# Eight v tiles of the second batch move into unused columns of the q and k buffers, and are loaded earlier

## The chip, the cores and the metric

The kernel runs on one core of a Trainium2 chip. The metric is the time of one execution on the device in microseconds (us). Three executions of the kernel before took 538.85, 540.19 and 541.0 us; the median, 540.19, is the time before.

## The reference

Three stages, each feeding the next. Inputs are random normal numbers; most are scaled up by 8.

```python
# attention: B=2, H=8, S=768, D=64; block 32, window 16
k_sum = k.reshape(B, H, 24, 32, D).max(axis=3)
v_sum = v.reshape(B, H, 24, 32, D).mean(axis=3)
scores_l = q @ k^T / 8, kept where |i - j| < 16
scores_s = q @ k_sum^T / 8 + log(32)
a = softmax([scores_l, scores_s]);  x = a @ [v, v_sum]      # -> 1536 x 512
# experts: 8 of them, 512 -> 1024 -> 512; one per token
do = x @ w_skip > 0;  e = argmax(x @ w_gate);  g = softmax(x @ w_gate)[e]
x[do] += g * (relu(x @ w1[e]) @ w2[e])
# feed-forward 512 -> 2048 -> 512
h = x @ w_in;  out = (h >= 1 ? h : h <= -1 ? 0 : (h + 1)^2 / 4) @ w_out
```

## The kernel before, in words

**Stages.** The program first does the attention with the routing of the tokens (`attention`), which goes on into the block of the first expert; then the other experts; then the feed-forward layer. In attention every engine executes its instructions in the order in which the code lists them. Buffers are guarded by semaphores that the framework derives from the regions read and written: an instruction waits for the earlier ones that touch what it touches.

**Attention units.** The 24 units of attention are counted through both batches: 0 to 11 for batch 1 (index b = 0 in the code), 12 to 23 for batch 2 (b = 1). A unit is one token tile of 128 queries and half of the heads. A token tile t consists of two blocks j = 2t and 2t + 1 of 64 queries, each with a window of 96 keys (64 of its own and 16 at either side) and 24 block sums. So unit 18 (batch 2, t = 3, first half of the heads) and unit 19 read v tiles 6 and 7 of batch 2. In batch 1 the first six units go through tiles 0, 1, 2 twice.

In step i of the loop TensorE transposes the probabilities of unit i + 1 (`stage_t`, L449), makes the scores of unit i + 3 (`stage_s`, L437), and multiplies the probabilities of unit i by v (`stage_pv`, L466, tile `xo`). VectorE takes the row maximum of the scores (`nm`, L439), ScalarE the exponentials (`p`, L442), ScalarE copies the transposed probabilities (`pts`, L451), VectorE divides by the sum and writes the token tile (`den`, L469; `x`, L471). Then `run_todo(i)` (L780) issues what the table `todo` lists for step i: loads, routing of a finished token tile (`r1` to `r5`), weight fetches and pieces of weight splits.

**v tiles.** A v tile holds 120 rows (96 keys, 24 block sums) by 8 heads by 66 columns: 64 of v, two that are 1 for the keys and 32 for the sums, whose product is the divisor. `load_v` (L381, its DMA is L385) loads the keys of one tile from `v`, 192 KB; it is issued by SP. There are NV = 6 buffers `vw`; tile j of either batch goes to `vw[j % 6]`, so that each load after the first six waits for the last unit that reads the buffer's old tile. In batch 1 the block sums are put there by `spread` (L370). For batch 2 they go through DRAM: `store_vs` (L373, GpSimd) writes them to `vs_d`, and `put_vs` (L375, its DMA is L376, SP) copies them into a tile's last 24 rows. That is done for the first six tiles of batch 2; the other six find the same sums in their buffer. The v loads of batch 2 stand at steps 8 to 19, one per step.

**q and k.** Each pair of heads of each batch has a buffer `pb` of 2976 columns for its q and k blocks; its zeros are set by `init_pair`. These buffers have the places ("w00" to "w13") which later hold the split expert weights, of 4096 columns each. Pairs 4 to 7, of batch 2, have "w10" to "w13".

**SP's queue.** SP issues all of these loads in the order of the code; when one has to wait for a buffer, those behind it wait too. For batch 2 its order around the change is: a v load and a copy of sums per step; at step 11 a register load (`top_reg`) of a number that VectorE works out at step 10; at steps 12 to 15 the four fetches of the first expert's weights (`fetch`, L129, 1 MB each) behind the v load of that step; at steps 18 and 19 the list of the first block's tokens (`load_ids`, L216) and the gather of their rows on GpSimd (L219); at steps 20 to 22 the next expert's fetches.

**Routing.** A finished token tile gets its places in the experts' lists; GpSimd scatters indices (`ids_d`, L556) and rows (`xf`, L224) to DRAM. The tokens live in a ring of 7 buffers `x`, so a new tile's first write (L471) waits for the scatter of the tile seven places earlier. The split of a weight (`hi` on ScalarE, L139; `lo` on VectorE, L145) is done in pieces in steps 15 to 24.

Of the kernel before, what the change touches and what calls it, by code (L numbers as in the profile page):

```python
# [8 lines left out]
F32 = mybir.dt.float32  # L9
# [15 lines left out]
NV = 6  # L25
# [15 lines left out]
def tile_net(ctx, tc, q, k, v, w_skip, w_gate, w1, w2, w_in, w_out, out):  # L41
    nc = tc.nc
# [3 lines left out]
    NT = B * S // 128  # L46
    cp = ctx.enter_context(tc.tile_pool(name="cons", bufs=1))
    wp = ctx.enter_context(tc.tile_pool(name="w", bufs=1))
# [236 lines left out]
    def attention(actx):  # L285
# [24 lines left out]
                masks.append(m)  # L310


        pb = {}
        for i, tag in enumerate(("w02", "w03", "w00", "w01", "w10", "w11", "w12", "w13")):
            t = wp.tile([128, 2976], F32, tag=tag, name=f"pb{i}")
            pb[i] = t[:, 0:1536].rearrange("p (j c) -> p j c", c=128), t[:, 1536:2976].rearrange("p (j c) -> p j c", c=120)
        vw = [per.tile([120, 8, 66], F32, name=f"vw{i}") for i in range(NV)]

        def init_pair(eng, i):
            tq, tk = pb[i]  # L320
            eng.memset(tq[0:64, :, 64:128], 0.0)
            eng.memset(tq[64:128, :, 0:64], 0.0)
            eng.memset(tk[:, 0, 0:16], 0.0)
            eng.memset(tk[:, 11, 80:96], 0.0)

        def pbuf(b, hp):
            return pb[4 * b + hp]
# [45 lines left out]
            nc.gpsimd.dma_start(out=vs_d[96 * c:96 * c + 96], in_=vs[c])  # L373

        def put_vs(b, j, hs=slice(0, 8)):  # L375
            nc.sync.dma_start(out=vw[j % NV][96:120, hs],  # L376
                              in_=vs_d.rearrange("(b h n) d -> b n h d", b=B, h=H)[b, :, hs])

        vtile = {}

        def load_v(b, j):  # L381
            t = vw[j % NV]
            lo, hi = max(0, 64 * j - 16), min(S, 64 * j + 80)
            r0 = lo - (64 * j - 16)
            nc.sync.dma_start(out=t[r0:r0 + hi - lo, :, 0:64], in_=v[b, :, lo:hi].rearrange("h s d -> s h d"))  # L385
            vtile[b, j] = t
# [35 lines left out]
        def units(i):  # L422
            b, t, a = i // 12, (i % 12) // 2, i % 2
            if i < 6:
                t, a = i % 3, i // 3
            return b, t, a, [(2 * a + c, 2 * t + e) for c in range(2) for e in range(2)]

        def stage_s(i):
            b, _, _, us = units(i)
            s = ps.tile([128, 4, 120], F32, tag="s", name="s", bufs=3)  # L430
            t = units(i)[1]
            mask = masks[1 if t == 0 else 2 if t == 5 else 0]
            nc.tensor.matmul(s.rearrange("p (c e) k -> p c e k", c=2), identb,
                             mask.unsqueeze(1).to_broadcast([128, 2, 2, 120]), start=True, stop=False)
            for u, (hp, j) in enumerate(us):
                tq, tk = pbuf(b, hp)
                nc.tensor.matmul(s[:, u], tq[:, j], tk[:, j], start=False, stop=u == 3)  # L437
            nm = wk.tile([128, 4], F32, tag="nm", name="nm", bufs=3)
            nc.vector.tensor_reduce(out=nm, in_=s, axis=AX.X, op=ALU.max, negate=True)  # L439
            p = wk.tile([128, 4, 120], F32, tag="p", name="p")  # L440
            for u in range(4):
                nc.scalar.activation(out=p[:, u], in_=s[:, u], func=AF.Exp, bias=nm[:, u:u + 1], scale=1.0)  # L442
            st["p", i] = p
# [12 lines left out]
        def stage_pv(i):  # L456
            b, t, a, us = units(i)
            pts = st.pop(("t", i))
            tt = 6 * b + t
            if a == 0:  # L460
                xt[tt] = next(xnext)
            xo = ps.tile([128, 4, 66], F32, tag="xo", name="xo", bufs=2)
            for u, (hp, j) in enumerate(us):
                par = j % 2
                for h in range(2):
                    nc.tensor.matmul(xo[64 * par:64 * par + 64, 2 * (u // 2) + h], pts[:, u, 64 * h:64 * h + 64],  # L466
                                     vtile[b, j][:, 2 * hp + h, :], start=True, stop=True)
            den = wk.tile([128, 4], F32, tag="den", name="den")
            nc.vector.tensor_scalar(out=den, in0=xo[:, :, 64], scalar1=1e-9, scalar2=None, op0=ALU.add)  # L469
            nc.vector.reciprocal(out=den, in_=den)  # L470
            nc.vector.tensor_tensor(out=xt[tt][:, 256 * a:256 * a + 256].rearrange("p (s d) -> p s d", d=64),  # L471
                                    in0=xo[:, :, 0:64], in1=den.unsqueeze(2).to_broadcast([128, 4, 64]), op=ALU.mult)
# [257 lines left out]
        def at(i, f, *a):  # L730
            todo[i].append(lambda: f(*a))

        for t in range(3, NT):
            for e in range(2):
                b, j = t // 6, 2 * (t % 6) + e
                i = 2 * t - 4 + (e or t == 3)
                at(i, load_v, b, j)
                if b and j < NV:
                    at(i, put_vs, 1, j)
        groups = {2: (0, 1, 2), 5: (3, 4, 5), 6: (6,), 8: (7, 8), 10: (9, 10), 11: (11,)}  # L740
        of = {t: g for g in groups.values() for t in g}
        for t in range(NT):
            i = 2 * t + 1 if t > 2 else t + 3
# [49 lines left out]

        load_qk(0, 0), load_qk(0, 1)
        load_v(0, 0)
        load_vsum(0)
        load_v(0, 1)
        load_qk(0, 2)
        load_v(0, 2)
# [46 lines left out]
        route_consts(tri, per.tile([128, E * CAP // 128 + 2], I32, name="sent"), per.tile([128, 8], I32, name="ii"))  # L846
        for i in range(4, 8):
            init_pair(nc.gpsimd, i)
        stage_s(3)
        stage_pv(2)  # L850
        stage_s(4)
# [16 lines left out]
        t, = end = groups[NT - 1]  # L868
# [455 lines left out]
    with ExitStack() as actx:  # L1324
        with tc.manual_schedule():
            attention(actx)
# [38 lines left out]
```

## Time and profile before

| | |
|---|---|
| three executions | 538.85, 540.19, 541.0 us |
| the profiled execution | 538.99 us, its span 537.3 us |
| TensorE busy | 492.9 us (92%) |
| VectorE busy | 356.4 us (66%) |
| ScalarE busy | 286.1 us (53%) |
| GpSimd busy | 109.9 us (20%) |
| mean granted TensorE clock | 0.961 |

The profiled execution is one run; the span goes from its first to its last instruction, and its own time is 1.7 us longer. An engine's busy time is a mean over stages of different kinds: attention takes roughly the first 130 us, the experts follow to about 250, the feed-forward layer is the rest. In the rows below, PE is TensorE, DVE is VectorE, ACT is ScalarE, POOL is GpSimd, and SPq is the queue of SP. A clock of 1.00 is TensorE at full speed.

### The profile page before, as it was taken

How to read it: one execution, taken by the hardware profiler on the slowest of the kernel's cores; microseconds unless marked ns; L12 is line 12 of the kernel's file. 1: busy time of each engine (PE TensorE's matmuls, PEld its weight loads, DVE VectorE, ACT ScalarE, POOL GpSimd, SP SyncE). 2: the span in 40 equal slices, each digit the busy share in tenths (PEclk: the TensorE clock that was granted, in tenths of full speed). 3: DMA queues.
4: the chain of work that ended last, by engine and by line, in shares of the span. 5: the costliest groups of instructions: out<-in, count | busy, mean ns of one | idle time of the engine just before them, and what ended most of it. 6: DMA issues, size and time to landing. Idle time of an engine off the chain costs nothing.

```text
span 537.3 us, 7783 instructions
## 1 busy us (share of the span) xinstructions
PE 492.9 (92%) x2742; PEld 401.2 (75%) x2742; DVE 356.4 (66%) x714; ACT 286.1 (53%) x512; POOL 109.9 (20%) x159
## 2 busy tenths in 40 slices
PE   6887979687989999986899999999999999999994
PEld 3676868586778888854678888888888888888883
DVE  6667675869588879989989999543333444333341
ACT  6575546563457686773567777633233343332341
POOL 8506431603544231332000000020000002000002
PEclk9799999877889999999899999999999999999998
DMA  9997517997289887998425566020000002000002
GB/s 206 224 211 182 102 38 185 237 248 206 70 296 364 277 290 264 314 342 309 160 78 205 192 230 220 21 80 0 1 0 1 0 1 79 1 0 1 1 0 84
DMA packets 66760, 76.83 MB, mean 143 GB/s; under 512 B 31046, under 2 KB 48486, under 8 KB 66328
## 3 DMA queue, kind: packets, MB, share of 16 engines
q1 hardware_dynamic: 63256, 67.99, 43.1%
q0 software_dynamic: 3456, 8.26, 4.6%
q8 instruction: 23, 0.38, 0.3%
q14 instruction: 25, 0.20, 0.2%
HBM read 69.55 MB, written 8.12 MB: 145 GB/s over the span
## 4 chain that ended last, share of the span: by engine, by line
PE 43%; issue 33%; DVE 12%; ACT 6%; DMA 3%; POOL 1%; SPq 1%; POOLq 0%; ACTq 0%; DVEq 0%
PE hf L1146 9%; PE hp L935 5%; PE yp L959 5%; PE o L1189 3%; PE o L1187 3%; PE s L437 3%; PE o L1188 3%; DMA vw<-in_v_dram 3%; DVE w L145 3%; PE tph L945 2%; PE hp L264 2%; POOL out_dram L1199 1%; PE xo L466 1%; PE pt L449 1%; PE lp L492 1%
## 5 line engine op out<-in xcount | busy, mean ns | idle before, releaser
L1146 PE MATMUL hf<-xh,w 128*128 128x512 f32 x384 | 128.3, 397 | 1.2 <-ACT xh L257 0.7
L1146 PEld LDWEIGHTS hf<-xh,w 128*128 128x128 f32 x384 | 72.5, 190 | 18.0 <-ACT w L1111 1.0
L145 DVE TENSOR_TENSOR w<-stg,w 128x1024 fp32r<-128x1024 f32 (+1 forms) x72 | 76.5, 1096 | 6.8 <-ACT w L139 6.8
L1187 PE MATMUL o<-w,g 128*128 128x512 f32 x192 | 77.2, 402 | 2.2 <-ACT g L1171 2.2
L1188 PE MATMUL o<-w,g 128*128 128x512 f32 x192 | 76.5, 398 | 0.0
L1146 PE MATMUL hf<-xl,w 128*128 128x512 f32 x192 | 75.5, 393 | 0.0
L1189 PE MATMUL o<-w,g 128*128 128x512 f32 x192 | 71.3, 399 | 0.0
L139 ACT CAST w<-stg 128x1024 fp32r<-128x1024 f32 (+1 forms) x72 | 65.0, 958 | 3.1 <-PE hp L935 1.5
L1156 ACT ACTIVATE c<-c,scal 128x512 f32<-128x512 f32 x32 | 23.2, 724 | 76.7 <-DVE c L1155 76.6
L1199 POOL DMA_INDIRECT out_dram<-ob,perm x12 | 11.8, 983 | 254.2 <-DVE ob L1198 165.0
L1166 DVE TENSOR_TENSOR hf<-hf,c 128x512 f32<-128x512 f32 x48 | 33.5, 698 | 39.5 <-ACT hf L1164 37.7
L1155 DVE TENSOR_SCALAR c<-hf 128x512 f32<-128x512 f32 x32 | 22.1, 692 | 42.2 <-PE hf L1146 42.2
L1172 DVE TENSOR_TENSOR g<-hf,g 128x512 fp32r<-128x512 f32 x48 | 33.1, 690 | 22.7 <-ACT g L1171 22.6
L1187 PEld LDWEIGHTS o<-w,g 128*128 128x128 f32 x192 | 36.4, 189 | 10.8 <-ACT g L1171 2.7
L1171 ACT CAST g<-hf 128x512 fp32r<-128x512 f32 x48 | 28.1, 586 | 28.4 <-DVE hf L1166 28.2
L1189 PEld LDWEIGHTS o<-w,g 128*128 128x128 f32 x192 | 36.6, 191 | 8.7
L1146 PEld LDWEIGHTS hf<-xl,w 128*128 128x128 f32 x192 | 36.3, 189 | 8.8 <-DVE xl L258 0.7
L1188 PEld LDWEIGHTS o<-w,g 128*128 128x128 f32 x192 | 36.7, 191 | 8.3
L442 ACT ACTIVATE p<-s,nm 128x120 f32<-128x120 f32 x96 | 26.8, 362 | 29.3 <-DVE nm L439 21.3
L224 POOL DMA_INDIRECT xf<-x,ids x10 | 24.6, 2456 | 64.5 <-DVE x L967 63.3
L959 PE MATMUL yp<-w,hT 128*128 128x512 f32 x128 | 34.6, 407 | 2.3 <-DVE w L145 2.3
L935 PE MATMUL hp<-w,xT 128*128 128x512 f32 x128 | 34.2, 416 | 2.1 <-DVE xT L924 1.3
(211 smaller groups left out, 825.1 us busy)
## 6 DMA issues: line engine op xcount, KB each, us to landing
stg<-in_moe_w_dram SPq DMA_DIRECT2D x32, 1024.0 KB, 7.6
raw<-in_moe_w_in_dram SPq DMA_DIRECT2D x14, 512.0 KB, 3.7
raw<-in_moe_w_out_dram SPq DMA_DIRECT2D x14, 512.0 KB
vw<-in_v_dram SPq DMA_DIRECT2D x20, 192.0 KB, 6.0
x<-xf SPq DMA_DIRECT2D x12, 264.0 KB, 6.2
raw<-in_k_dram SPq DMA_DIRECT2D x16, 192.0 KB, 3.9
raw<-in_q_dram SPq DMA_DIRECT2D x16, 192.0 KB, 4.2
vraw<-in_v_dram SPq DMA_DIRECT2D x4, 768.0 KB, 9.0
```

The lines of the kernel that those rows point to most:

```text
L139: copy(out=part(wset[p, c // 2][0], c % 2, i, pieces), in_=part(stage[p, c], 0, i, pieces))
L145: eng.tensor_tensor(out=lo, in0=part(stage[p, c], 0, i, pieces), in1=hi.bitcast(F32), op=ALU.subtract)
L442: nc.scalar.activation(out=p[:, u], in_=s[:, u], func=AF.Exp, bias=nm[:, u:u + 1], scale=1.0)
L935: nc.tensor.matmul(hp, xT[:, kk], w[:, kk, 512 * f:512 * f + 512], start=(kk == 0 and w is hi), stop=(kk == 3 and w is lo))
L959: nc.tensor.matmul(yp, hT[:, kk], w[:, kk], start=(kk == 0 and w is hi), stop=(kk == 7 and w is lo))
L1146: nc.tensor.matmul(hp, w[:, 128 * kk:128 * kk + 128], a[:, kk], start=(n == 0), stop=(n == 11))
L1166: nc.vector.tensor_tensor(out=hp, in0=hp, in1=c, op=ALU.add)
L1171: nc.scalar.copy(out=gh, in_=hp)
L1172: nc.vector.tensor_tensor(out=gl, in0=hp, in1=gh.bitcast(F32), op=ALU.subtract)
L1187: nc.tensor.matmul(ops[ch][t], gh[:, a], hi, start=(f == 0), stop=False)
L1188: nc.tensor.matmul(ops[ch][t], gh[:, a], lo, start=False, stop=False)
L1189: nc.tensor.matmul(ops[ch][t], gl[:, a], hi, start=False, stop=(f == NF - 1))
```

## The change

The buffers of pairs 4 to 7 grow from 2976 to 4032 columns. Each of these four tails holds two v tiles, so there are eight more. Tiles 0 to 7 of batch 2 go to the tails (those of pairs 6 and 7 first), tiles 8 to 11 to `vw[0]` to `vw[3]`. `init_tails`, on GpSimd right behind `init_pair` of the same buffers, sets the columns of ones in all eight and 16 rows of zeros in tile 0. The v loads of batch 2 stand at step 5 (tiles 0 and 1), 6 (2, 3), 7 (4, 5), 8 (6 to 9) and 10 (10, 11). All twelve tiles get their sums by `put_vs`, three tiles at each of steps 8 to 11. Batch 1 keeps its buffers and the steps of its loads.

```diff
-        pb = {}
+        pb, tails = {}, []
         for i, tag in enumerate(("w02", "w03", "w00", "w01", "w10", "w11", "w12", "w13")):
-            t = wp.tile([128, 2976], F32, tag=tag, name=f"pb{i}")
+            t = wp.tile([128, 4032 if i > 3 else 2976], F32, tag=tag, name=f"pb{i}")
             pb[i] = ...
+            if i > 3:
+                tails += [t[0:120, 2976 + 528 * n:3504 + 528 * n].rearrange("p (h d) -> p h d", d=66) for n in range(2)]
         vw = [per.tile([120, 8, 66], F32, name=f"vw{i}") for i in range(NV)]
+        vbuf = {(0, j): vw[j % NV] for j in range(12)}
+        vbuf.update({(1, j): (tails[4:] + tails[:4] + vw)[j] for j in range(12)})
+
+        def init_tails():
+            for t in tails:
+                nc.gpsimd.memset(t[0:96, :, 64:66], 1.0)
+            nc.gpsimd.memset(vbuf[1, 0][0:16], 0.0)
...
-            nc.sync.dma_start(out=vw[j % NV][96:120, hs],
+            nc.sync.dma_start(out=vbuf[b, j][96:120, hs],
...
-            t = vw[j % NV]
+            t = vbuf[b, j]
...
-        for t in range(3, NT):
+        for t in range(3, 6):
             for e in range(2):
-                b, j = t // 6, 2 * (t % 6) + e
-                i = 2 * t - 4 + (e or t == 3)
-                at(i, load_v, b, j)
-                if b and j < NV:
-                    at(i, put_vs, 1, j)
+                at(2 * t - 4 + (e or t == 3), load_v, 0, 2 * t + e)
+        for j in range(12):
+            at(5 + j // 2 if j < 8 else 6 + (j - 8) // 2 * 2 + 2, load_v, 1, j)
+            at(8 + j // 3, put_vs, 1, j)
...
         for i in range(4, 8):
             init_pair(nc.gpsimd, i)
+        init_tails()
```

## Rows read from the trace of the kernel before

**Rows 1.** The chain of waits, 76 to 160 us: start, us, what.
```profile
94.25 14.19 DMA vw<-in_v_dram
```
**Rows 2.** Timeline of TensorE, 60 to 150: start, us, instructions [idle before <-releaser].
```profile
103.83 0.42 PE L466 MATMUL xo<-vw,pts 120*64 120x66 f32 x4
108.48 1.14 PE L466 MATMUL xo<-vw,pts 120*64 120x66 f32 x12 [4.24 <-DMA vw<-in_v_dram]
...
111.72 1.79 PE L437 MATMUL s<-pb 128*128 128x120 f32 x8
...
128.29 1.06 PE L256 MATMUL tpx<-ident,x 128*128 128x128 f32 x4
```
**Rows 3.** Timeline of SP's queue, 0 to 160.
```profile
52.54 8.96 SPq L385 DMA_DIRECT2D vw<-in_v_dram  x4
...
80.29 0.32 SPq L385 DMA_DIRECT2D vw<-in_v_dram  x1
80.69 0.50 SPq L376 DMA_DIRECT2D vw<-vs_d  x1
...
99.33 10.54 SPq L385 DMA_DIRECT2D vw<-in_v_dram  x3
```
**Rows 4.** DMA issues, windows 61.5-62.5, 79-80.5, 98-101, 101-104, 151-152: us to landing last.
```profile
vw<-in_v_dram SPq DMA_DIRECT2D x1, 192.0 KB, 3.5
...
xf<-x,slot POOLq DMA_INDIRECT x1, 9.7
...
vw<-in_v_dram SPq DMA_DIRECT2D x2, 192.0 KB, 16.6
...
xf<-x,slot POOLq DMA_INDIRECT x1, 11.5
ids_d<-slot,si POOLq DMA_INDIRECT x1, 10.8
...
x<-xf,ids POOLq DMA_INDIRECT x1, 9.7
```
**Rows 5.** Timeline of VectorE, 80 to 155.
```profile
89.73 0.42 DVE L471 TENSOR_TENSOR x<-xo,den 128x256 f32<-128x256 f32 x1 [1.34 <-DMA xf<-x,slot]
...
106.34 0.64 DVE L439 TENSOR_REDUCE nm<-s 128x4 f32<-128x480 f32 x1
109.66 0.16 DVE L469 TENSOR_SCALAR den<-xo 128x4 f32<-128x4 f32 x1 [2.69 <-PE xo L466]
...
113.55 0.66 DVE L439 TENSOR_REDUCE nm<-s 128x4 f32<-128x480 f32 x1 [1.85 <-PE s L437]
...
116.78 0.66 DVE L439 TENSOR_REDUCE nm<-s 128x4 f32<-128x480 f32 x1 [0.20 <-PE s L437]
```
**Rows 6.** Stretches: us, busy time of each engine, granted clock, DMA share, GB/s.
```profile
50.00:80.00 30.00, 26.61 (x295) 23.93 (x294) 22.37 (x81) 15.04 (x41) 12.95 (x22) 1.00 0.41 84
62.00:64.00 2.00, 2.00 (x19) 1.98 (x19) 0.71 (x2) 1.79 (x5) 0.00 (x0) 1.00 0.71 159
88.00:90.00 2.00, 2.00 (x17) 1.88 (x17) 0.63 (x4) 1.12 (x4) 0.00 (x0) 1.00 0.99 385
160.00:180.00 20.00, 20.00 (x108) 16.40 (x107) 16.75 (x18) 13.60 (x20) 7.96 (x6) 1.00 0.95 342
```
**Rows 7.** Timeline of GpSimd, 0 to 160.
```profile
4.83 0.53 POOL L808 MEMSET vw<- 16x528 f32 x1
...
43.47 0.33 POOL L414 COPY pb<-pb 128x176 f32<-128x176 f32 x1 [22.59 <-DVE pb L399]
...
79.90 0.98 POOL L224 DMA_INDIRECT xf<-x,slot  x1 [0.31 <-issue]
...
103.59 0.98 POOL L556 DMA_INDIRECT ids_d<-slot,si  x1 [0.30 <-DVE den L470]
...
118.71 1.07 POOL L219 DMA_INDIRECT x<-xf,ids  x1 [12.85 <-PE pt L449]
```
**Rows 8.** Timeline of ScalarE, 80 to 155.
```profile
110.76 0.59 ACT L483 COPY xs<-tpx 128x512 f32<-128x512 f32 x1 [2.58 <-PE tpx L482]
```

## The prediction

> **What bounds the kernel now.** I read the page first, then the chain of waits from 76 to 160 us, then the timelines of the engines around its largest piece, and the landing times of DMAs last. In the chain the reader is to see one piece that no engine computes: a v load, issued at 94.25 us, that takes 14.19 us to land [rows 1]. By counting the attention units back from the last one, this is the load of v tile 7 of batch 2; unit 18 is the first to use it. TensorE does that unit's matmuls on tile 6 at 103.83, then stands 4.24 us until 108.48 [rows 2]. The load is late because it stands in SP's one queue: SP reached v tile 4 only at 80.29, after a register load, and from there each v load alternates with a 1 MB fetch of expert weights; the next three v loads keep SP from 99.33 to 109.87 [rows 3]. A v load with nothing in front takes 3.5 us, the rest is queueing [rows 4].
>
> VectorE is the other half of the picture. It works without a gap from 89.73 to 106.98 (end of the row-maximum instruction that starts at 106.34), so TensorE's stall costs only what VectorE then misses: 2.69 us before 109.66, 1.85 before 113.55 and 0.20 before 116.78; of other idle there is 0.15 [rows 5]. That is 4.9 us. The middle piece is an echo: after the stall TensorE's granted clock fell to 0.5 (its 1.2 GHz level; 1.0 is 2.4) and eight score matmuls took 1.79 us, against 1.05 at full clock elsewhere in the same timeline [rows 2]. From 116.78 to 131.05 VectorE has next to no idle and sets the pace; then follow the first expert's block and the experts, where TensorE is busy in all of 160 to 180 [rows 5, 6]. Nothing after 131 hangs on a fixed time, so what is won before 131 should arrive at the end.
>
> **The change part by part.**
>
> *The loads of tiles 0 to 7.* They wait for no attention unit any more. Tiles 0 to 5 are issued at units 5 to 7, 6 and 7 at unit 8. SP stands at unit 5 at 52.54, where it spends 8.96 us, largely waiting, on four v loads [rows 3]; the new loads go into that wait, behind the last q and k load and behind tile 9 of batch 1, in order, so nothing that is needed sooner is pushed back by them except tiles 10 and 11 of batch 1, needed at 74.76 in TensorE's timeline, some 15 us later.
>
> *The transfers themselves.* Eight loads (4 to 11) move from behind 80 us to before it, and there are six more small copies of the block sums (12 instead of 6). From 50 to 80 the DMA engines are busy 0.41 of the 30 us, so 17.7 us are free; one load and two such copies made 0.71 of 2 us, so a load with a copy costs at most 1.4 us [rows 6]. Eight times that is 11 us: it fits.
>
> *The added waits.* The copies for tiles 0 to 7 wait for the stored sums, whose last store leaves GpSimd at 57.81 in its timeline. Behind them on SP stand the loads of tiles 6 to 11 and then the register load. The loads of 8 and 9 wait for unit 7, of 10 and 11 for unit 9, over by 70.3 us in TensorE's timeline; SP is free of all this by about 74. The register load before 80.29 waited for VectorE's value anyway, so it isn't later. Cost: nothing, with 6 us of cover.
>
> *GpSimd.* Eight memsets of 96x16 (0.12 us, one every 0.15 in the row of such) and one of 16x528 at 0.53: 1.7 us. GpSimd then has 22.59 us of idle before 43.47 [rows 7]. Cost: nothing.
>
> *The fetches.* With no v load between them the four fetches follow the register load at about 80.3, one behind the other. 385 GB/s, as from 88 to 90 [rows 6], is 2.7 us for one and 10.9 us for four: all has landed by about 95, where before the last was issued at 95.18 in SP's timeline. Nobody waits for them: the first split of a weight on ScalarE is a step of unit 15, and TensorE was just then busy.
>
> *The scatter that shares those engines.* VectorE's write at 89.73 had waited 1.34 us for the scatter of token tile 0, issued at 79.90 [rows 5, 7], because it reuses that tile's buffer. From there VectorE is gapless, so whatever this scatter gains or loses counts in full. Its landing took 9.7 us; a scatter issued amid the fetches took 11.5 [rows 4]. Bounds: 1.3 us won (the whole wait gone; below that the units before set the end) to 1.8 us lost. Two v loads and two copies leave its neighbourhood, and fetches come in their place. I take 0.5 us lost, nearer to the row of the same scatter than to the loaded one.
>
> By the Trainium skill, "DMA: Bandwidth & Descriptors", section "Queues, rings and completion order", a DMA engine goes round the queues packet by packet and drains a whole packet of about 9 to 17 descriptors before it switches. A fetch is 256 rows of 4 KB, 16 on each engine, so by this rule the scatter may stand behind one whole fetch. The difference between the landings above, 1.8 us, is smaller than a fetch's 2.7 but doesn't refute it. By the rule the loss would be 2.7 instead of 0.5; that result is the second case below.
>
> *Unit 18 to 20 without the stall.* From 106.98 I set the next steps behind one another with the durations of rows. ScalarE: exponentials of unit 21 to 108.2; its next step stood 2.58 us for a transpose [rows 8] that TensorE now has done by 105.2, so copy, two casts and the copy for unit 20 follow to 110.4. TensorE then has a transpose of 0.5 and the scores of unit 23 of 1.1, to 112.0. VectorE's row maximum starts there, instead of at 116.78: 4.8 us earlier, 0.1 less than its whole idle. If only the first wait went and the half clock stayed it would be 2.7.
>
> *The sum.* 4.8 - 0.5 = 4.3 us. The profiled execution itself took 538.99 us (a span of 537.3 and 1.7 around it), 1.2 under the median of 540.19. So 534.7 against itself, and 535.9 against the median, which I give as the time.
>
> **Rivals.**
>
> *The scatter stands behind a whole fetch* (2.7 us): 4.8 - 2.7 = 2.1 won, 538.1. For it: VectorE did wait for this scatter, and the fetches now begin right behind it. Against: only 1.8 us between the landings measured with and without fetches.
>
> *The gather takes over.* Before the first expert block its rows are gathered: scatter of indices at 103.59, landing 10.8 us later, index load on SP 4.3 us before the gather at 118.71, first transpose of the gathered rows on TensorE at 128.29 [rows 2, 4, 7]. TensorE didn't wait there, but a gather under load took 9.7 [rows 4], and 118.71 + 9.7 = 128.4: it may have been just in time. If this chain doesn't move up, nothing is won: 540.2. Against: the fetches and v loads that slowed the index scatter will be over. At the page's medians, 7.2 us for an index scatter and 4.5 for a gather, with the same 4.3 between them, it lands at 103.59 + 0.5 + 7.2 + 4.3 + 4.5, about 120, and is needed at 124.
>
> *Slower: the scatters wait until all four fetches have drained.* The place is the same VectorE write; the price is up to the 10.9 us above, so 4.8 - 10.9 = 6.1 lost, 546.3. It decides against the change when the scatter lands over 4.8 us later than at 89.6, and shows as slower from 7.5. For it: a v load behind fetches did take 16.6 us [rows 4]. Against: that load is in the same queue as the fetches, the scatter is in GpSimd's, and there 11.5 was the longest of this stretch.
>
> *The change does not do what it says:* the new v tiles share buffers with q and k, and if order were kept for a whole buffer, score matmuls would wait for loads into its unused columns. The first reader is unit 12 at 69 us. Each such wait is at most a load's 3.5 us, and two of them beside waits that are there now would leave about 2: 538. Against: the copy into tile 4 left SP 0.4 us after the load into the same buffer [rows 3] and the load itself took 8.5 to land, so writes to other rows of one buffer don't wait for one another.
>
> **How the numbers follow.** Forecast 0.58, scatter behind one fetch 0.14, gather 0.14, slower 0.07, whole-buffer order 0.07. A difference of 0.5%, 2.7 us, is about what a measurement of this kernel can tell from no change. Faster by more: 0.54 of the forecast's 0.58, and 0.09 from near misses of the others, 0.63. Slower by more: 0.06 of the slower case and 0.02 of the rest, 0.08. Within: 0.29. Lowest: all 4.9, the scatter's 1.3, and 1.5 from a granted clock that falls less between 126 and 137, where it was 0.5 to 0.7: 532.5. Highest: the gather's case with a little noise, 540.5. The forecast's own range is 533.5 to 537.5.
>
> **What would show it.** Right: no wait of TensorE for a v tile; the first matmul of unit 18 on tile 7 follows tile 6 at once; VectorE's maximum of unit 23 some 4 us earlier; SP with four fetches in a row from about 80; GpSimd's nine memsets near 21 to 23, with nobody behind. The scatter's landing and VectorE's wait for it near 90 decide between the first two cases, TensorE's idle before the first transpose of gathered rows the third. Wrong: VectorE's write after 91.5, a gather landing after 124, or expert blocks that lose again what the attention won.

## The result and the profile after

| | before | after |
|---|---|---|
| median of 20 executions each, same chip (A) | 540.16 us (534.8 to 543.15) | 534.5 us (531.25 to 540.09) |
| the profiled execution, its span | 538.99, 537.3 us | 536.4, 534.7 us |
| mean granted clock of the profiled execution | 0.961 | 0.962 |

The ratio after to before is 0.9918, with a 95% interval of 0.9893 to 0.9943: 4.4 us won (0.0082 times 540.16). The medians lie 5.7 apart, inside that interval (3.1 to 5.8 us); the ratio, unlike the medians, leaves disturbed executions out. The forecast was 4.3. The pair of profiled executions shows less, 2.6 us, and why is a part of the lesson.

The wait for the v tile is gone. TensorE's timeline after, the PV matmuls of units 17 to 20, answers to [rows 2]:

```profile
103.37 1.20 PE L475 MATMUL xo<-pb,pts 120*64 120x66 f32 x16
...
107.10 0.74 PE L475 MATMUL xo<-pb,pts 120*64 120x66 f32 x16
...
108.90 1.05 PE L446 MATMUL s<-pb 128*128 128x120 f32 x8
109.88 0.74 PE L475 MATMUL xo<-pb,pts 120*64 120x66 f32 x16
...
113.91 0.74 PE L475 MATMUL xo<-vw,pts 120*64 120x66 f32 x16
```

Unit 18 runs its 16 matmuls in one piece. It starts 3.27 us later than before, but unit 19 starts at 109.88 instead of 113.44. The score matmuls ahead of unit 19 take 1.05 us (108.90), where before they took 1.79 (111.72): the half clock behind the stall went with it.

The queue of SP after, which answers to [rows 3]:

```profile
52.75 2.45 SPq L394 DMA_DIRECT2D pb<-in_v_dram  x2
...
72.44 1.31 SPq L385 DMA_DIRECT2D vw<-vs_d  x3
79.80 3.78 SPq L129 DMA_DIRECT2D stg<-in_moe_w_dram  x4
109.28 0.35 SPq L216 DMA_DIRECT2D ids<-ids_d  x1
```

All loads and copies are issued by 73.75 and the four fetches follow the register load in one run. GpSimd, which answers to [rows 7]: the nine memsets, and the next work behind them, which still stands 21 us for VectorE.

```profile
20.85 0.43 POOL L325 MEMSET pb<- 96x16 f32 x8
21.23 0.53 POOL L326 MEMSET pb<- 16x528 f32 x1
...
42.84 0.33 POOL L423 COPY pb<-pb 128x176 f32<-128x176 f32 x1 [21.08 <-DVE pb L408]
```

VectorE after, which answers to [rows 5], and under it the DMA issues of 79 to 80 and 104.5 to 105.5 us, which answer to [rows 4]:

```profile
91.08 0.42 DVE L480 TENSOR_TENSOR x<-xo,den 128x256 f32<-128x256 f32 x1 [2.15 <-DMA xf<-x,slot]
...
108.34 0.64 DVE L448 TENSOR_REDUCE nm<-s 128x4 f32<-128x480 f32 x1
...
110.83 0.65 DVE L448 TENSOR_REDUCE nm<-s 128x4 f32<-128x480 f32 x1
...
114.01 0.66 DVE L448 TENSOR_REDUCE nm<-s 128x4 f32<-128x480 f32 x1 [0.47 <-PE s L446]
```

```profile
xf<-x,slot POOLq DMA_INDIRECT x1, 11.7
...
ids_d<-slot,si POOLq DMA_INDIRECT x1, 4.3
```

Two terms of the sum can be read here, and one that it lacks. From the row maximum of unit 21 to that of unit 23 it is 5.67 us (108.34 to 114.01), before 10.44: 4.77 won, forecast 4.8. The write that waits for the scatter of token tile 0 comes 1.35 later than before, forecast 0.5. The scatter lands in 11.7 us instead of 9.7. The term that the sum lacks is 0.65: from the row maximum of unit 20 to that of unit 21 VectorE needs 4.64 us (103.70 to 108.34) instead of 3.99 (102.35 to 106.34). TensorE's granted clock was 0.66 in 100 to 105 us, where before it was 1.00 in 99 to 104, and VectorE waits for it twice, 0.27 and 0.19 us. So the row maximum of unit 23 comes 4.77 - 1.35 - 0.65 = 2.77 us earlier (114.01 against 116.78), not the "some 4" that were to show the forecast right.

Stretches after (us; busy TensorE, weight load, VectorE, ScalarE, GpSimd; granted clock, DMA share, GB/s). The first answers to the first of [rows 6]:

```profile
50.00:80.00 30.00, 28.40 (x284) 25.54 (x283) 22.72 (x82) 15.62 (x44) 13.31 (x22) 0.89 0.92 145
70.00:78.00 8.00, 7.97 (x52) 7.16 (x51) 5.72 (x31) 3.82 (x12) 2.10 (x3) 0.57 0.75 90
126.00:137.00 11.00, 10.29 (x46) 8.03 (x45) 6.86 (x45) 2.49 (x6) 5.28 (x6) 0.73 0.48 174
```

The last of them in the kernel before:

```profile
126.00:137.00 11.00, 10.19 (x42) 8.11 (x43) 9.44 (x55) 1.60 (x4) 5.36 (x6) 0.54 0.62 144
```

And TensorE at the first expert after, where it waits for gathered rows; under it the same place before, where it waits about as long for VectorE:

```profile
145.08 0.43 PE L929 MATMUL tpx<-ident,x 64*128 64x64 f32 x4 [1.65 <-DMA x<-xf,ids]
145.89 0.69 PE L929 MATMUL tpx<-ident,x 64*128 64x64 f32 x4 [0.38 <-DMA x<-xf,ids]
146.51 6.66 PE L944 MATMUL hp<-w,xT 128*128 128x512 f32 x16
```

```profile
148.18 0.71 PE L920 MATMUL tpx<-ident,x 64*128 64x64 f32 x8 [0.85 <-DVE x L281]
150.14 5.54 PE L935 MATMUL hp<-w,xT 128*128 128x512 f32 x16 [1.25 <-DVE xT L924]
```

The ledger of the two profiles, as starts on TensorE after minus before: -0.64 at unit 9; +0.97 at unit 11, behind the 70 to 78 us in which the clock was 0.57 (before: 1.00); +0.54 at unit 15; +3.27 at unit 18, of which the scatter's 1.35 is a part; -3.56 at unit 19; -2.77 at unit 23; -3.88 behind the first layer of the first block (136.10 against 139.98), since in 126 to 137 us the clock is 0.73, before 0.54; -3.63 at the first expert (146.51 against 150.14), when the 2.03 us of waiting for gathered rows are already paid, against 2.10 of waiting for VectorE before; -2.50 behind its first 16 matmuls (155.87 against 158.37), which take 6.66 us instead of 5.54 at a granted clock of 0.55 (146.5 to 153); -1.9 at the last matmul.

### The profile page after: what moved, and what is told of

It is laid out like the page before. It is cut to its first block, busy times and chain, and to the rows that moved or that the text cites. A ratio compares the mean times of both kernels' runs of the same rounds, so it can differ in the third digit from the quotient of the medians.

```text
span 534.7 us, 7791 instructions
## 1 busy us (share of the span) xinstructions
PE 493.8 (92%) x2742; PEld 402.9 (75%) x2742; DVE 355.6 (67%) x714; ACT 285.6 (53%) x512; POOL 111.2 (21%) x168
## 4 chain that ended last, share of the span: by engine, by line
PE 39%; issue 34%; DVE 15%; ACT 6%; DMA 4%; POOL 2%; POOLq 0%; SPq 0%; ACTq 0%; DVEq 0%
PE hf L1155 7%; PE hp L944 5%; PE yp L968 5%; DVE w L145 3%; PE tph L954 2%; PE o L1198 2%; PE o L1196 2%; DMA xf<-x,slot 2%; PE o L1197 2%; PE yp L280 2%; PE hp L264 2%; PE s L446 2%; ACT pb L416 1%; DVE nm L448 1%; POOL out_dram L1208 1%
## 5 line engine op out<-in xcount | busy, mean ns | idle before, releaser
L1196 PEld LDWEIGHTS o<-w,g 128*128 128x128 f32 x192 | 36.4, 189 | 10.7 <-ACT g L1180 2.7
L224 POOL DMA_INDIRECT xf<-x,ids x10 | 27.3, 2731 | 64.8 <-DVE x L976 63.6
L944 PE MATMUL hp<-w,xT 128*128 128x512 f32 x128 | 35.4, 427 | 0.8 <-DVE w L145 0.8
```

What stands on the lines that cost most here:

```text
L224: return nc.gpsimd.indirect_dma_start(out=xf[:, :], out_offset=bass.IndirectOffsetOnAxis(ap=ids, axis=0), in_=xg.bitcast(I32), in_offset=N ...
L944: nc.tensor.matmul(hp, xT[:, kk], w[:, kk, 512 * f:512 * f + 512], start=(kk == 0 and w is hi), stop=(kk == 3 and w is lo))
L1196: nc.tensor.matmul(ops[ch][t], gh[:, a], hi, start=(f == 0), stop=False)
```

## The experiments

The first theory: the gain is the wait for v tile 7, and it goes because SP issues that load before the fetches. Its rivals: a buffer of its own is enough, the issue doesn't matter; and the scatter's loss is larger than forecast, so that a version without it is better by 2 us. The four chips are called A (the result above), B, C and D; the kernel before ran beside each of them.

**The change as it is, on chip C.** Expected: 

> The changed kernel as it is, once more, for a second profile and a second ratio. Theory (the stall of 4.24 us at unit 18 is gone, some 2 us of it are paid back where VectorE waits longer for the scatter of token tile 0): the ratio to the kernel before is again near 0.992, so 534 to 537 us; in the profile no wait of TensorE for a v tile, and VectorE's write of token tile 7 waits 2 us or more for the scatter. The lower granted clock at 70 to 78 us is chance and need not come again. Rival (the clock at 70 to 78 belongs to the change): it is low again at the same place and unit 11 is again 1 to 1.6 us later than before.

Measured: 545.71 us, the kernel before 545.14; ratio 0.9995 (0.9960 to 1.0029). A miss: no gain. VectorE and TensorE in this trace:

```profile
88.17 0.16 DVE L478 TENSOR_SCALAR den<-xo 128x4 f32<-128x4 f32 x1 [4.66 <-remote]
```

```profile
83.85 1.05 PE L446 MATMUL s<-pb 128*128 128x120 f32 x8
89.11 0.71 PE L475 MATMUL xo<-pb,pts 120*64 120x66 f32 x16 [4.21 <-remote]
```

Both engines stand together, for nothing that the program names ("remote" is no buffer of it). Units 12 to 18 come 7.2 to 12.5 us later than in the kernel before on chip A, 3.6 of which it has already at unit 6. Whether the kernel before has this on chip C too was open at that point; the three edits that ran beside it can tell little for the same reason.

**The new buffers with the old issue, on chip C.** The v loads and copies of batch 2 go back to steps 8 to 19.

```diff
-        for t in range(3, 6):
+        for t in range(3, NT):
...
+                b, j = t // 6, 2 * (t % 6) + e
+                i = 2 * t - 4 + (e or t == 3)
+                at(i, load_v, b, j)
+                if b:
+                    at(i, put_vs, 1, j)
```

Expected: 

> The eight tails stay, but the v loads of batch 2 go back to steps 8 to 19, one per step, each with its copy of sums behind it. Theory (what held tile 7 back was SP waiting for buffers between the fetches): with free buffers SP runs ahead anyway, tile 7's load is issued within some 5 us of the first fetch and lands by 96 instead of 108; no stall at unit 18; 535 to 537, the same as the changed kernel within 1.5 us. Rival (the early issue is what counts, a load behind fetches is late whatever its buffer): tile 7 or 8 lands after its unit is due, TensorE waits 2 to 4 us, 538 to 541.

Measured: 545.37, ratio 0.9992 (0.9957 to 1.0027). Inconclusive where the change itself wins nothing; it was run again on chip D, below.

**Only tiles 6 and 7 in new buffers, on chip C.** Loaded with their copies at step 8; all else as in the kernel before.

```diff
-        vbuf.update({(1, j): (tails[4:] + tails[:4] + vw)[j] for j in range(12)})
+        vbuf.update({(1, j): tails[j - 2] if j in (6, 7) else vw[j % NV] for j in range(12)})
...
+                if b and j in (6, 7):
+                    at(8, load_v, b, j), at(8, put_vs, b, j)
+                    continue
```

Expected: 

> Only tiles 6 and 7 of batch 2 live in tails and are loaded at step 8; the other ten keep the six buffers and the steps of the kernel before. Theory (one load, tile 7's, was late, and it alone made the stall): the stall at unit 18 is gone, 535 to 537. Rival (the next load takes its place): SP still stands for units 11, 13 and 15 between the fetches, so tiles 8 and 9 are behind the fetches in turn and TensorE waits for them at unit 20; at least 2 us of the 4.2 come back, 538 to 540.

Measured: 545.16, ratio 1.0007 (0.9961 to 1.0053). Inconclusive.

**An eighth place for token tiles, on chip C.** Token tile 7 goes into v buffer 4, which the changed kernel no longer needs by then, so VectorE's write waits for no scatter.

```diff
-        vw = [per.tile([120, 8, 66], F32, name=f"vw{i}") for i in range(NV)]
+        full = [per.tile([128, 8, 66], F32, name=f"vw{i}") for i in range(NV)]
+        vw = [t[0:120] for t in full]
+        spare = full[4].rearrange("p h d -> p (h d)")
...
-                xt[tt] = next(xnext)
+                xt[tt] = spare if tt == 7 else next(xnext)
...
+        at(12, nc.gpsimd.memset, spare[:, 514:XW], 0.0)
```

Expected: 

> The changed kernel, with token tile 7 in the v buffer 4, which batch 2 no longer uses, so that its first write waits for no scatter; the ring of seven buffers then serves the others, one place longer. Theory (the wait of 2.15 us at that write is on the path): the write comes at about 89 instead of 91, what follows is 1.5 to 2.2 us earlier, 532.3 to 533.5, a ratio to the kernel before near 0.988. Rival (units 12 to 15 on TensorE set the end there, or the clock takes it back): the wait is gone, but unit 20 is where it was within 0.7 us, and the time within 1 us of the changed kernel.

Measured: 546.57, ratio 0.9985 (0.9949 to 1.0022): nothing that can be told from no change.

**The kernel before, profiled on chip B.** Expected: 

> The kernel before as it is, for its profile on the chip of this set of runs. On the chip of the first set every kernel took 545 us or more, the changed one gained nothing there, and its profile showed two things that the first pair of traces didn't have: a low granted clock from 50 to 59 us, and VectorE standing 4.66 us near 84 us for nothing that the profile names. Theory (both belong to the chip; units 12 to 18 come later there, so tile 7 is no longer late in the kernel before): if the chip is such a one, this profile has the same two stretches and no wait, or a wait under 1 us, for tile 7 at unit 18. Rival (VectorE's stand belongs to the change, which puts four fetches in front of it): this profile has the wait for tile 7 of about 4 us and no stand of VectorE near 84. If the chip is like the first one: a wait of 3 to 5 us for tile 7, as in the rows of before.

Measured: 540.13 us, and the waits are there, 3.3 us in two pieces on TensorE, besides 0.67 at unit 16 for a copy of sums:

```profile
107.66 1.07 PE L466 MATMUL xo<-vw,pts 120*64 120x66 f32 x12 [2.84 <-DMA vw<-in_v_dram]
...
115.76 1.17 PE L466 MATMUL xo<-vw,pts 120*64 120x66 f32 x16 [0.48 <-DMA vw<-in_v_dram]
```

Its row for 70 to 78 us shows the low clock, so that is not something that the change brings:

```profile
70.00:78.00 8.00, 8.00 (x52) 7.42 (x53) 5.74 (x30) 3.79 (x12) 2.07 (x2) 0.57 0.29 62
```

**The changed kernel on chip B.** Expected: 

> The changed kernel as it is, on the same chip as the profile of the kernel before. Theory: the ratio goes with the wait for tile 7 in that profile: about 0.992 where the wait is 3 to 5 us, 0.998 to 1.002 where it is under 1 us. Rival (the first ratio was luck): 1.0 even where the kernel before waits 3 us or more for tile 7.

Measured: ratio 0.9957 (0.9916 to 0.9998), that is 2.3 us won, though only just clear of nothing (0.1 to 4.5), and the medians, 540.7 and 540.5, don't show it. No wait for v; the scatter lands in 9.0 us and VectorE doesn't wait for it. Unit 20 starts at 112.94 instead of 115.76, and unit 23 3.82 us earlier (120.06 against 123.88). But in its profiled execution all is lost again at the gathers of the first expert's rows, which run beside fetches. TensorE, then SP's queue:

```profile
145.26 0.66 PE L929 MATMUL tpx<-ident,x 64*128 64x64 f32 x4 [2.89 <-DMA x<-xf,ids]
150.78 0.68 PE L929 MATMUL tpx<-ident,x 64*128 64x64 f32 x4 [4.86 <-DMA x<-xf,ids]
```

```profile
143.88 10.30 SPq L129 DMA_DIRECT2D stg<-in_moe_w_dram  x3
```

That is 7.75 us of waiting here, 2.03 in the changed kernel's profile on chip A, 1.97 in the kernel before on chip B. The first expert's matmuls then start at 151.39, 1.96 later than in the kernel before on this chip.

**The eighth place on chip B.** Same edit. Expected: 

> The changed kernel with token tile 7 in a buffer of its own, so that its first write waits for no scatter. Theory (the wait for the scatter is on the path where VectorE doesn't stand before it): 1.5 to 2.2 us less than the changed kernel in this set if that one's profile shows a wait of about 2 us for the scatter; within 1 us of it if it shows none. Rival: within 1 us of it in either case.

Measured: 534.7 us, ratio 0.9892 (0.9838 to 0.9946), the lowest of all, though its interval overlaps those of its neighbours. By the ratios that is 3.5 us below the changed kernel, where the expectation gave under 1, since the changed kernel's profile here has no wait for the scatter: a miss. What can be read is that this profile waits 5.8 us less for gathered rows; that the eighth place brings this about isn't shown. The write goes to the free buffer and waits for nothing, while the scatter took 11.3 us. VectorE, then TensorE at the first expert, where 1.96 us of waiting are left:

```profile
88.37 0.42 DVE L482 TENSOR_TENSOR vw<-xo,den 128x256 f32<-128x256 f32 x1
```

```profile
143.10 0.43 PE L932 MATMUL tpx<-ident,x 64*128 64x64 f32 x4 [1.72 <-DMA x<-xf,ids]
143.78 0.57 PE L932 MATMUL tpx<-ident,x 64*128 64x64 f32 x4 [0.24 <-DMA x<-xf,ids]
```

**The fetches held until that scatter has landed, on chip B.** A load of 8 bytes into unused columns of token tile 0, ahead of the four fetches, waits for the scatter.

```diff
+        at(12, lambda: nc.sync.dma_start(out=xring[0][0:1, 514:516], in_=q[0, 0, 0:1, 0:2]))
```

Expected: 

> The changed kernel with the four fetches held on SP until the scatter of token tile 0 has landed (an 8-byte load into a padding column of its buffer stands before them). Theory (the fetches slow the scatter down): the scatter of token tile 0 lands in under 9.7 us instead of 11.7, VectorE's write of token tile 7 waits less than 0.5 us, the fetches start at 86 to 90 and still land before their splits, and the time is 1 to 2 us below the changed kernel. If VectorE stands near 84 in the changed kernel because of the fetches, that goes too, and up to 4.7 us more are won. Rival (the first indirect DMAs are slow by themselves): the scatter lands in 9.5 to 12 us as before, the wait stays 1.5 us or more, and the time is the same within 1 us, or later where the splits then wait for the fetches.

Measured: 536.59, ratio 0.9919 (0.9885 to 0.9953). SP's queue, and the scatter's issue at 82 to 82.5:

```profile
90.60 0.28 SPq L781 DMA_DIRECT2D x<-in_q_dram  x1
91.15 2.35 SPq L129 DMA_DIRECT2D stg<-in_moe_w_dram  x4
```

```profile
xf<-x,slot POOLq DMA_INDIRECT x1, 8.4
```

The fetches go out 11 us later than in the changed kernel on chip A, and nobody waits for them. The scatter, with no fetch beside it, takes 8.4 us. The ratio is 2 us below the changed kernel's, but the intervals overlap, and the changed kernel's profile on this chip didn't wait for the scatter either: that holding the fetches wins anything isn't shown.

**The kernel before, profiled on chip D.** Expected: 

> The kernel before, for its profile on the chip of the next three. Expected if the wait for v tile 7 is the cost that the change takes away: TensorE stands 2 to 5 us before the PV matmuls of unit 18 on tile 7 (4.24 and 2.84 so far). If this chip is one where VectorE stands 4 to 5 us near 88 us for something that the profile doesn't name, and units 12 to 18 come later by 9 us, then tile 7 is no longer late here and that wait is under 1 us: then the gain must be missing from the next three too.

Measured: 541.26 us (median of the kernel before on this chip: 544.65). This shows for chip D why there is nothing to win; for chip C, where the kernel before wasn't profiled, it is an inference. TensorE:

```profile
82.58 0.47 PE L437 MATMUL s<-pb 128*128 128x120 f32 x2 [0.47 <-issue]
84.02 0.38 PE L437 MATMUL s<-pb 128*128 128x120 f32 x2 [0.97 <-issue]
...
108.82 0.17 PE L492 MATMUL lp<-wg,xs 128*128 128x9 f32 x1 [0.86 <-issue]
109.55 0.17 PE L492 MATMUL lp<-wg,xs 128*128 128x9 f32 x1 [0.56 <-issue]
...
114.11 1.20 PE L466 MATMUL xo<-vw,pts 120*64 120x66 f32 x16
```

SP's queue, the load of tile 7:

```profile
92.89 0.60 SPq L385 DMA_DIRECT2D vw<-in_v_dram  x1
```

The kernel before has no wait for a v tile at all here. Its engines stand in places that the program doesn't name, unit 18 comes at 114.11, 10.3 later than on chip A, while SP issues tile 7 at 92.89, 1.4 earlier. What the change takes away is not there to be taken, in this one execution at least.

**The old issue again, on chip D.** Expected: 

> The eight added buffers stay, but the v loads and copies of batch 2 stand at steps 8 to 19 again, so between the fetches. Theory (the early issue is the gain): SP reaches tile 7 about 13 us after the first fetch, as in the kernel before, TensorE waits 2 to 4 us for it, ratio to the kernel before 0.997 to 1.003. Rival (the own buffer is enough, since no load waits for an attention unit any more): no wait, ratio near the changed kernel's 0.992 to 0.996.

Measured: 546.5, ratio 1.0035 (0.9998 to 1.0072). SP's queue, from the first fetch to tile 7:

```profile
82.36 2.09 SPq L129 DMA_DIRECT2D stg<-in_moe_w_dram  x1
84.50 0.98 SPq L394 DMA_DIRECT2D pb<-in_v_dram  x1
85.53 1.96 SPq L385 DMA_DIRECT2D pb<-vs_d  x1
87.74 0.72 SPq L129 DMA_DIRECT2D stg<-in_moe_w_dram  x1
88.50 2.37 SPq L394 DMA_DIRECT2D pb<-in_v_dram  x1
90.91 3.20 SPq L385 DMA_DIRECT2D pb<-vs_d  x1
94.35 0.40 SPq L129 DMA_DIRECT2D stg<-in_moe_w_dram  x1
94.80 0.51 SPq L394 DMA_DIRECT2D pb<-in_v_dram  x1
```

No load here waits for an attention unit, and still tile 7 is issued 12.4 us after the first fetch, against 12.8 in the kernel before on chip A (94.25 less 81.45, where its first fetch is issued) and 7.6 in the kernel before on this chip (92.89 less 85.27). Issuing itself holds SP: a copy of 50 KB takes 2.0 to 3.2 us to issue behind fetches, 0.4 or so in the three at 72.44 above. In the kernel before on chip A 4.7 of the 12.8 us are waits for buffers (0.3, 1.8 and 2.6); here there are none, and the time goes to issues. One of them, the 3.20 at 90.91, is the copy of sums that tile 6 needs only because its buffer is new. So with these buffers the old steps don't bring tile 7 forward; the earlier place in the queue does. TensorE's wait isn't in this trace, since unit 18 comes at 115.89 on this chip; that it would come back where tile 7 is late was not shown: neither this edit nor the one with two tiles ran on A or B.

**Tiles 6 and 7 alone, on chip D.** Expected: 

> Only tiles 6 and 7 have new buffers and are loaded at step 8; the other v loads of batch 2 stand as before, between the fetches. Theory (the wait for tile 7 is the whole of the gain): no wait at unit 18, units 20 to 23 earlier by about 3 to 4 us, ratio 0.992 to 0.996. Rival (the next loads in SP's queue are late in their turn): TensorE waits 2 to 4 us for tile 8 to 10 at unit 19 to 21 and the ratio is 0.997 to 1.001.

Measured: 545.44, ratio 1.0003 (0.9961 to 1.0046). No v wait, as in the kernel before here; whether two tiles would give the whole gain on chip A stays open.

**The eighth place on chip D.** Expected: 

> The changed kernel with an eighth place for token tiles (v buffer 4, free by then), so that VectorE's write of token tile 7 waits for no scatter. If the scatter's later landing is a real loss in the changed kernel: no wait of VectorE at that write and 1 to 2 us better than the changed kernel's 0.992 to 0.996, so 0.988 to 0.993. If the scatter's wait is covered by what comes later (the gathers of the first expert's rows): 0.992 to 0.996, and the wait at the first transposes of gathered rows is longer by what was won.

Measured: 545.13, ratio 0.9999 (0.9966 to 1.0032). The whole change with the scatter's wait taken out wins nothing where the kernel before has no wait for v. In the two profiles unit 23 is 1.05 us earlier (127.28 against 128.33), and the first expert's second group of matmuls 1.08 later (160.47 against 159.39), since the first group takes 5.54 us instead of 3.98.

## Why the prediction was right, step by step

**The stall.** Right in place, cause and size: 4.77 us of 4.8. The reason that the sum didn't use TensorE's 4.24 but VectorE's idle held: VectorE was the engine that set the pace on both sides, and the half clock behind the stall, forecast to go, went. The chips give a counter-test: where the kernel before waits 4.24 us for tile 7 (A) or 3.3 for tiles of v (B), the change wins; on D, where its profile has no such wait, the change with the eighth place wins 0 within 0.4%. On C the change wins 0 within 0.4% too, but whether the wait is absent there was not seen.

**The loads, the waits, GpSimd.** Nobody waits for them, as forecast. The price of the transfers was too low: the DMA share of 50 to 80 us rose from 0.41 to 0.92, 15.3 us of DMA time and not at most 11. The bound came from one stretch of 2 us in which a load stood alone, and the share counts the time of packets that stand beside others (it can pass 1, as the 1.27 at the end of this document shows). The transfers fitted into the 17.7 that were free.

**The fetches.** In a row, and nobody waits. Their landing was forecast for 95; the one that the trace tells took 20.3 us, to about 102. The estimate took 385 GB/s for all of the time. In the profile after, 78 to 84 us moved 25 GB/s at a DMA share of 0.81. Nearly all of that share is SP's own queue, 79.9% of the 16 engines' time for 36 packets and 0.15 MB; the scatters' queue has 1.0%. So the fetches' own packets took long there, and why is open:

```profile
78.00:84.00 6.00, 6.00 (x72) 5.59 (x71) 3.56 (x13) 3.53 (x11) 3.90 (x4) 1.00 0.81 25
```

Held 11 us longer, the fetches landed in 10.8 to 16.7 us and nobody waited, so this error had no price.

**The scatter.** The mis-sized term: 0.5 forecast, 1.35 measured at VectorE on chip A (2.0 in the landing, of which 0.64 was covered because it was issued that much earlier). It lies within the bounds (1.3 won to 1.8 lost), and the value taken was too near to the row that knew fewer fetches. Landings of this scatter: 8.4 without fetches behind it, 9.7 and 9.4 with fetches and v loads in turn, 11.7, 9.0 and 11.3 with four fetches at once. The three with four fetches at once are 10.7 in the mean, 1.1 more than the kernel before's two and 2.3 more than the one without. By the Trainium skill, "DMA: Bandwidth & Descriptors", section "Queues, rings and completion order", a queue's packet is drained whole before the next queue's turn. With a whole fetch as that turn, 2.7 us, the landing would be 8.4 + 2.7 = 11.1, an estimate, inside what was seen. The runs neither show the packets' order nor refute it, but what the profile counts as a packet of these fetches is 4 KB, so a whole fetch is a high price for one turn. On chip B the unit before set the end and the scatter cost nothing.

**What arrives at the end.** "What is won before 131 should arrive at the end" is the step that the pair of profiles doesn't bear out as it was meant. By unit 23 the attention had won 2.77 us, not 4.3: 4.77 less the scatter's 1.35 and the 0.65 at the lower clock, which the sum put at nothing. From there on the granted clock moved the gain both ways: 1.1 more in 126 to 137 us (0.73 against 0.54), 1.1 less at the first expert's first 16 matmuls (6.66 us against 5.54). The wait for gathered rows cost next to nothing in this pair, since the kernel before stood as long for VectorE. On chip B it did cost: there the attention had won 3.82 at unit 23, and 7.75 us of waiting for gathered rows took all of it in that execution. This is the gather rival in another place: the first block's gather, which the prediction weighed, landed in 4.7 us and held nobody, but the next gathers, issued on GpSimd around 140 to 147 beside the next fetches, are waited for by nothing to 7.75 us from one execution to another. That the timed gain is 4.4, close to the 4.3 of a sum whose terms come to less in the profile, is in part luck. It may be the mean over such draws and over those of the clock, which differ much: in the 20 executions after, the time goes from 531.25 us at a mean clock of 0.976 to 540.09 at 0.945. No run takes the 4.4 apart.

**The rivals.** No whole-buffer order: units 12 to 19 never wait for a load into a tail. (The first reader, the scores of unit 12, comes at 66.89 before and not at 69; that changed nothing.) No scatter behind all four fetches: VectorE's write came at 91.08, before the 91.5 that was to refute the forecast, and the landing was 2.0 longer, not over 4.8. What no rival held is that the wait may not exist: on chip D the kernel before has none, and on chip C the change wins nothing either.

## What to carry to other kernels

Look first at where a late transfer's issue stands in the queue: in these runs each issue on SP took time of its own once large fetches were queued, so that free buffers at the old steps brought nothing forward. Price a removed stall by the idle time of the engine that sets the pace on both sides of it, then look for the next transfer that is only just in time, because it can take back part of the gain, and for stretches at a lower clock, which here moved the gain of one pair of profiles by 1 us either way. And look at the kernel before on more than one chip before promising a gain that hangs on a race between two engines: the race may have another winner there.

## What was not expected of the hardware

- Four chips, one program: the kernel before takes 540.2 and 540.5 us on A and B, 545.1 and 544.7 on C and D. In all eight profiles of C and D, one of them the kernel before, VectorE stands for 0.9 to 4.7 us between 79 and 90 us for something that the trace gives as "remote", and VectorE or TensorE again between 103 and 117 for "remote" or "issue"; in 78 to 125 us the six profiles of A and B have neither on these two engines. In the changed kernel on chip C, in 84 to 88 us, the DMA engines were busy all the time and moved little, nearly all of it in SP's queue (32 packets, 0.13 MB):

```profile
84.00:88.00 4.00, 0.89 (x9) 0.71 (x7) 0.00 (x0) 0.73 (x3) 2.43 (x3) 1.00 1.27 33
```

  Whether the two hang together, and what the engines stand for, is open; no run tests it.
- The spread of executions of one kernel goes with the granted clock: a line through the executions of a kernel on one chip gives 2 to 4.4 us less for 0.01 more of mean clock, in all kernels whose clocks are listed. Where the clock falls (70 to 78 us at 0.57 in some, 48 to 60 us in others) differs from run to run in both kernels.
- One index scatter landed in 4.3 us after, when fetches and v loads were over, and in 10.8 among them before [rows 4]. The scatter of token tile 0 took 9.0 to 11.7 us with fetches near it and still 8.4 with none, so the fetches are not the whole of its time.
